# Joined record loads at the ends of both rounds, 384 more key columns kept, and small tiles put together, in a two-round decode kernel

## The chip, the core and the metric

The kernel runs on one core of a Trainium2 chip. The metric is the device time of one execution in microseconds (us); less is better. The time before is 711.71 us, the median of 3 runs (711.58 to 711.9).

The engines in the text: PE (TensorE, matrix products; its weight loads are PEld), DVE (VectorE), ACT (ScalarE), POOL (GpSimd), and SP, which here only issues transfers from HBM. The 16 DMA engines of the core carry them out in the order of issue.

## The reference

Four layers of decode for 4 sequences, one new token each: attention, MLP, attention, MLP, each with a layer norm ahead and a residual. Both attention layers read the same caches and weights, and so do both MLPs.

```python
def _A_ref(x, k_cache, v_cache, wq, wo):        # x 4 x 1 x 640, 32 heads of 128
    W = min(4096, max(256, Sk // 4))            # the last 1024 positions
    q = (x @ wq).reshape(B, Sq, Hq, Dh).transpose(0, 2, 1, 3)
    k, v = k_cache[:, :, Sk - W:, :], v_cache[:, :, Sk - W:, :]
    p = softmax(einsum("bhqd,bhkd->bhqk", q, k) * (Dh ** -0.5))
    o = einsum("bhqk,bhkd->bhqd", p, v)
    return o.transpose(0, 2, 1, 3).reshape(B, Sq, Hq * Dh) @ wo

def _B_ref(x, w1, w2):                          # 640 -> 1728 -> 640
    return maximum(x @ w1, 0) @ w2

x = x + _A_ref(layernorm(x), ...)
x = x + _B_ref(layernorm(x), ...)
x = x + _A_ref(layernorm(x), ...)
x = x + _B_ref(layernorm(x), ...)
```

All numbers are 32-bit floats.

## The kernel before

The host lays the data out as 32 records, one for each head: 128 partitions by 9,472 columns (REC). Columns 0 to 640 are the head's query weights (WQ), 640 to 4,736 the keys of the 4 sequences in two halves of 2,048 (K, VH), 4,736 to 8,832 the values (V), the last 640 the output weights (WO). A record is 4.85 MB, the 32 together 155 MB, and each of the two rounds (attention and MLP) reads them; SBUF holds little over five. MLP weights stand in an array of their own (`wm`): 8,640 columns of W1 in five blocks, then W2 in tiles of 160 columns.

SBUF is cut into `store` (five slots of a record, and FIRST = 2,176 columns ahead of them), `kept` and `ring`. In round 0 head h goes to slot h mod 5; the order is 0 to 31. Round 1 begins with heads 27 to 31, which are still in SBUF, and goes on with 0 to 26; the first FIRST columns of head 0 (its query weights and its first keys) also stay from round 0.

All loads are listed ahead, in one order (`items`), and SP issues them in that order. A load is issued as soon as all columns that it overwrites have been used: after each step `done` frees that step's columns and `pump` issues what has room. One load has one completion: a consumer of any of its columns waits for all of it. The sizes of the loads are written by hand:

- `GROUPS`: five heads in three loads (`FIVE`: 15,744, 15,872 and 15,744 columns); the last group of round 1, heads 19 to 23, in four (`LAST_FIVE`: 14,208, 14,208, 9,472, 9,472).
- `ending`: the last three heads of a round in pieces, query weights and keys (4,736 columns) apart from the values. In round 0 the WO parts of the last six heads come last of all.
- `MLP_RING`, `IN_RING`, `places`: the passage between the rounds, in which MLP weights go through `ring` and a parked part of the last slot (`park` copies 2,560 columns of head 31 to PSUM, `unpark` brings them back into the slot of head 27), and round 1's first loads go piecewise into whatever columns come free.
- `W1_SLOT`, `W2_SLOT`: the last MLP weights, into slots of round 1 that come free.

PE, DVE and ACT each keep the order in which the code is written (`InOrder`). One step of the loop over heads, with n counting and h the head: scores of the next head (8 matmuls into one of two `sc_ps` tiles), its maximum (DVE) and exponential (ACT), values of head h (8 matmuls into `o_ps`), `picks` (DVE: adds up the blocks of `o_ps`), query of the head after next (5 matmuls into `misc`), `output_T` (`t_ps`), `project` (4 matmuls into `acc`, the residual), then `weights` (DVE: transposes the exponentials into `wT`, the matmul operand). So a head's query is issued one step ahead of its scores and two ahead of its values. In the last step of a round, four filler matmuls (`busy`, `acc<-kept`) stand between the values of the third last head and the query of the last.

The MLP: five blocks of W1 (matmuls `sc_ps<-ring,xT` or `sc_ps<-store,xT`), the hidden layer through DVE (transposes, relu), then W2 (matmuls `acc<-...,scratch`). After the second MLP, DVE copies `acc` to SBUF and SP stores it.

## Time and profile before

| | |
|---|---|
| median of 3 runs | 711.71 us (711.58 to 711.9) |
| the profiled execution's own time | 712.25 us |
| its span in the profile | 710.5 us |
| PE busy | 513.0 us (72%) |
| DVE busy | 293.3 us (41%) |
| ACT busy | 99.7 us (14%) |
| moved | 301.96 MB, mean 425 GB/s |
| mean granted PE clock | 0.803 of full speed |

The span runs from the first to the last event of the profile; the time has 1.75 us more around it. Nearly all instructions are recorded by one helper, so lines of the code say little and groups are told by their tiles: `misc<-xT,store` is a query, `sc_ps<-store,qT` scores, `o_ps<-store,scratch` values. Each fp32 matmul shows as two records (x10 for the 5 of a query). In brackets behind a row stands the engine's idle time ahead of it and what ended it. PEclk is the share of full speed that PE was granted.

### The profile page before, as it was taken

The numbers are of one execution on the slowest core, as the hardware profiler recorded it, in microseconds if no ns is written. First come the engines' busy times: TensorE is split into PE (matmuls) and PEld (weight loads), VectorE is DVE, ScalarE is ACT, GpSimd is POOL, SyncE is SP. The second block draws the span as 40 slices with busy tenths as digits, with TensorE's granted clock in tenths as the row PEclk, the third lists the DMA queues.
The fourth block names the chain that finished last, engine by engine and source line by source line (L and its number), as shares of the span: only waits on it lengthen the run. The fifth ranks groups of instructions, "written<-read, shape, count | busy, mean of one in ns | idle before, by whom it ended". The sixth has DMA issues, their size and how long they took to land.

```text
span 710.5 us, 8480 instructions
## 1 busy us (share of the span) xinstructions
PE 513.0 (72%) x3722; PEld 214.0 (30%) x3722; DVE 293.3 (41%) x518; ACT 99.7 (14%) x210; POOL 1.1 (0%) x9
## 2 busy tenths in 40 slices
PE   0777586677584578869888999656584678686986
PEld 0332232232331223333323443222241232332322
DVE  3242353243342343435531775525162243453651
ACT  0110110011010110111120422101010011011110
POOL 0000000000000000000000000000000000000000
PEclk9977787677778776877999999968597677777989
DMA  9999999999999999999999999999999999999996
GB/s 398 439 416 447 425 435 443 414 439 450 418 435 441 424 437 421 423 439 423 430 398 403 412 426 433 445 435 437 431 435 426 438 436 430 432 432 416 433 425 281
DMA packets 12596, 301.96 MB, mean 425 GB/s; under 512 B 1408, under 2 KB 1552, under 8 KB 4624
## 3 DMA queue, kind: packets, MB, share of 16 engines
q1 hardware_dynamic: 12528, 301.42, 98.9%
q8 instruction: 29, 0.48, 0.2%
q14 instruction: 7, 0.06, 0.0%
q10 hardware_dynamic: 32, 0.01, 0.0%
HBM read 301.34 MB, written 0.08 MB: 424 GB/s over the span
## 4 chain that ended last, share of the span: by engine, by line
DMA 72%; PE 23%; DVE 4%; issue 1%; ACT 1%; ACTq 0%; SPq 0%; DVEq 0%
DMA store<-rec 65%; PE sc_ps L102 9%; PE o_ps L102 6%; DMA store<-wm 4%; PE acc L102 3%; PE misc L102 3%; DMA ring<-wm 2%; DVE scratch L102 2%; PE t_ps L102 1%; DVE o_ps L102 1%; ACT oTs L102 1%; DVE small L102 0%; DVE sc_ps L102 0%; ACT sc_ps L102 0%; ACTq L102 0%
## 5 line engine op out<-in xcount | busy, mean ns | idle before, releaser
L102 PE MATMUL sc_ps<-store,qT 128*32 128x512 f32 x1024 | 194.5, 849 | 35.7 <-DMA store<-rec 34.3
L102 PE MATMUL misc<-xT,store 128*128 128x4 f32 x620 | 95.6, 281 | 109.8 <-DMA store<-rec 109.8
L102 DVE TENSOR_REDUCE small<-sc_ps 128x1 f32<-128x1024 f32 x64 | 78.4, 1224 | 181.3 <-PE sc_ps L102 181.2
L102 PE MATMUL o_ps<-store,scratch 128*16 128x512 f32 x960 | 149.5, 701 | 1.7 <-DMA store<-rec 1.4
L102 PEld LDWEIGHTS misc<-xT,store 128*128 128x128 f32 x620 | 90.2, 227 | 166.6 <-DMA store<-rec 119.4
L102 ACT ACTIVATE sc_ps<-sc_ps,small 128x1024 f32<-128x1024 f32 x64 | 69.8, 1091 | 322.6 <-DVE small L102 322.6
L102 DVE STREAM_TRANSPOSE sc_ps<-sc_ps 128x1024 f32<-128x1024 f32 (+1 forms) x70 | 80.8, 1155 | 0.1
L102 PEld LDWEIGHTS sc_ps<-store,qT 128*32 128x32 f32 x1024 | 41.5, 139 | 112.4 <-issue 60.7
L102 PEld LDWEIGHTS o_ps<-store,scratch 128*16 128x16 f32 x960 | 33.8, 117 | 117.4 <-issue 107.8
L102 DVE TENSOR_TENSOR o_ps<-o_ps,of_block 128x512 f32<-128x512 f32 x62 | 43.3, 699 | 50.6 <-PE o_ps L102 50.6
L102 DVE TENSOR_TENSOR qT<-misc,rows 128x4 f32<-128x4 f32 x61 | 9.5, 155 | 112.9 <-PE misc L102 112.9
L102 PE MATMUL acc<-store,oTs 128*4 128x160 f32 x488 | 34.1, 363 | 17.0 <-ACT oTs L102 17.0
L102 DVE TENSOR_REDUCE scratch<-o_ps 128x128 f32<-128x512 f32 x62 | 42.9, 691 | 2.1
L102 ACT COPY oTs<-t_ps 128x4 f32<-128x4 f32 x59 | 9.6, 163 | 207.4 <-PE t_ps L102 207.4
L102 PE MATMUL t_ps<-rows,scratch 128*128 128x4 f32 x118 | 25.8, 289 | 11.3 <-DVE scratch L102 10.3
L102 PEld LDWEIGHTS t_ps<-rows,scratch 128*128 128x128 f32 x118 | 21.9, 231 | 17.4 <-DVE scratch L102 13.1
L102 DVE SCALAR_TENSOR_TENSOR scratch<-sc_ps,small,of_batch 128x128 f32<-128x128 f32 (+1 forms) x70 | 23.7, 339 | 3.5 <-PE o_ps L102 0.9
L102 PE MATMUL acc<-kept,small 128*1 128x328 f32 (+2 forms) x54 | 17.7, 433 | 0.0
L102 PEld LDWEIGHTS acc<-store,oTs 128*4 128x4 f32 x488 | 7.1, 84 | 22.5 <-ACT oTs L102 22.1
L102 ACT ACTIVATION_READ_ACCUMULATOR sc_ps<-sc_ps,small 128x1 f32 x64 | 12.3, 193 | 0.0
L102 DVE RECIPROCAL small<-small 128x1 f32<-128x1 f32 x64 | 9.8, 153 | 2.3 <-ACT sc_ps L102 2.3
L102 PE MATMUL acc<-store,scratch 128*4 128x160 f32 x146 | 6.1, 299 | 3.3 <-DMA store<-wm 3.2
(83 smaller groups left out, 99.8 us busy)
## 6 DMA issues: line engine op xcount, KB each, us to landing
store<-rec SPq DMA_DIRECT2D x14, 7872.0 KB, 27.3
store<-rec SPq DMA_DIRECT2D x7, 7936.0 KB, 29.9
store<-rec SPq DMA_DIRECT2D x4, 7104.0 KB, 30.8
store<-rec SPq DMA_DIRECT2D x11, 2368.0 KB, 36.5
store<-rec SPq DMA_DIRECT2D x3, 4736.0 KB, 25.7
store<-rec SPq DMA_DIRECT2D x2, 4416.0 KB, 29.1
store<-rec SPq DMA_DIRECT2D x3, 2048.0 KB, 40.7
store<-rec SPq DMA_DIRECT2D x1, 4160.0 KB, 21.6
```

What stands on the lines that cost most here:

```text
L102: r = build(*args, **kwargs)
```

## The change

Eight of 88 transfers go, by joins:

- Round 0, heads 25 and 26: the two records are stored interleaved in HBM (query weights and keys of 25, the same of 26, values and WO of 25, the same of 26), in both rounds. In round 0 the pair comes in one load up to column 16,256, with the rest of 26's values going to `kept` as before. Head 29 comes whole but for its WO.
- Round 1: heads 19 to 23 come as `FIVE`, 24 as one load, query weights and keys of 25 and 26 as one load. W1 of the second MLP comes in two loads instead of three.
- The passage: `unpark` lays the parked columns side by side, so that the free rest of head 27's keys is one stretch of 1,536 columns instead of 1,024 and 512; head 28's keys make room for one load of 4,096 instead of two of 2,048.

FIRST grows by 384 columns, paid for by smaller small tiles: `xT` keeps 32 columns, `scratch` 256; four tiles of four columns become `quads`. One score matmul of head 0 in round 1 is cut in two at the new border. The hidden layer is transposed inside PSUM and its used columns alone are written to `scratch`.

```diff
-FIRST = K + 3 * 512
+FIRST = K + 3 * 512 + 384
...
-IN_RING = [(2176, 4736, "spare", 0), (4736, 6272, "ring", 0), (6272, 8832, "ring", 1536)]
+IN_RING = [(FIRST, 4736, "spare", 0), (4736, 6272, "ring", 0), (6272, 8832, "ring", 1536)]
+PAIR = H - 7
+PAIRED = [(PAIR, 0, V, 0), (PAIR + 1, 0, V, V), (PAIR, V, REC, 2 * V), (PAIR + 1, V, REC, V + REC)]
-W1_SLOT = [[0, 1], [2, 3], [4]]
+W1_SLOT = [[0, 1, 2], [3, 4]]
-LAST_FIVE = [REC + 4736, 2 * REC - 4736, REC, REC]
-GROUPS = [{h: FIVE for h in range(0, 25, 5)}, {6: THREE, 9: FIVE, 14: FIVE, 19: LAST_FIVE}]
+GROUPS = [{h: FIVE for h in range(0, 25, 5)}, {6: THREE, 9: FIVE, 14: FIVE, 19: FIVE}]
...
-    xT = sb.tile([P, FD], F32, name="xT")
-    scratch = sb.tile([P, 480], F32, name="scratch")
+    xT = sb.tile([P, 32], F32, name="xT")
+    scratch = sb.tile([P, 256], F32, name="scratch")
...
+    def pair(r, lo, hi):
+        parts = [(("rec", r, h), x + max(lo - a, 0), min(y, x + hi - a), home(PAIR, r) + max(lo, a))
+                 for h, x, y, a in PAIRED if lo < a + y - x and a < hi]
+        load(rec, PAIR * REC + lo, PAIR * REC + hi, "store", home(PAIR, r) + lo, parts)
...
     def ending(r, hs, late):
         a, b, c = hs[-3:]
-        end = WO if late else REC
-        for h, lo, hi in ((a, 0, V), (b, 0, V), (a, V, end), (c, 0, V), (b, V, end), (c, V, WO if late else KEPT)):
-            piece(r, h, lo, hi)
-        if late:
+        if not late:
+            piece(r, a, 0, REC)
+            for lo, hi in ((0, 2 * V), (2 * V, V + REC), (V + REC, REC + KEPT)):
+                pair(r, lo, hi)
+        else:
+            for h, lo, hi in ((a, 0, WO), (b, 0, V), (c, 0, V), (b, V, WO), (c, V, WO)):
+                piece(r, h, lo, hi)
...
-        if h >= 25:
-            piece(0, h, 0, KEPT if h == LAST - 1 else WO if h >= H - LATE else REC)
-        if h == LAST - 1:
-            piece(0, h, KEPT, WO, "kept", 0)
+        if h == PAIR:
+            pair(0, 0, REC + KEPT)
+            piece(0, h + 1, KEPT, WO, "kept", 0)
+        elif h >= LAST:
+            piece(0, h, 0, WO)
...
-        a = b + (K, K + 512, K + VH, K + VH + 512, K + VH + 1024)[i]
+        a = b + K + 512 * i
...
-            dve.transpose(scratch[:, lo:hi], h_ps[:, lo:hi])
-            h = hT[:, lo // 32:hi // 32, :B]
+            dve.transpose(warm[:, lo:hi], h_ps[:, lo:hi])
+            h = warm[:, lo:hi].rearrange("p (m j) -> p m j", j=32)[:, :, :B]
...
+    rec[PAIR:PAIR + 2] = np.concatenate([rec[h, :, x:y] for h, x, y, _ in PAIRED], 1).reshape(P, 2, REC).swapaxes(0, 1)
```

How the loads stand on SP's queue at the end of round 1, before: heads 19 to 23 in four, then 24's keys, 25's keys, 24's values, 26's keys, 25's values, a part of 26's values, then the weights (a DMAHW name in a wait is a completion count of an earlier load, PE_49 a count of PE's steps).

```order
L102 DMA store<-rec 128x14208 [waits DMAHW3_49,PE_49]
L102 DMA store<-rec 128x14208 [waits DMAHW4_49,PE_49]
L102 DMA store<-rec 128x9472 [waits DMAHW5_49,PE_49]
L102 DMA store<-rec 128x9472 [waits PE_49]
L102 DMA store<-rec 128x4736 [waits DMAHW6_49]
L102 DMA store<-rec 128x4736 [waits PE_49] x2
L102 DMA store<-rec 128x4736 [waits DMAHW7_49,PE_49]
L102 DMA store<-rec 128x4736 [waits PE_49]
L102 DMA store<-rec 128x2048 [waits PE_49]
```

The same place now, from head 19's group on:

```order
L105 DMA store<-rec 128x15744 [waits DMAHW7_49,PE_49]
L105 DMA store<-rec 128x15872 [waits DMAHW0_49,PE_49]
L105 DMA store<-rec 128x15744 [waits DMAHW1_49,PE_49]
L105 DMA store<-rec 128x9472 [waits DMAHW2_49,PE_49]
L105 DMA store<-rec 128x9472 [waits DMAHW3_49,PE_49]
L105 DMA store<-rec 128x4736
L105 DMA store<-rec 128x2048 [waits PE_49]
```

The first 9,472 columns are head 24, the second the query weights and keys of 25 and 26 together; the columns in front of that load's end are the same as those in front of 26's keys before.

What PE does with them, before: the query of head 25 (the first `misc` row), with output and projection of head 23, 25's scores, 24's values, the fillers, the query of head 26 (`sc_ps_73` and `sc_ps_74` are the two score tiles, 70 and 71 in the changed kernel).

```order
L102 MATMUL misc<-xT,store 128x4 [waits DMAHW3_49]
L102 MATMUL t_ps<-rows,scratch 128x4 [waits DVE_49]
L102 MATMUL acc<-store,oTs 4x160 [waits Activation_49]
L102 MATMUL sc_ps_73<-store,qT 32x512 [waits DVE_49]
L102 MATMUL o_ps<-store,scratch 16x512 [waits DMAHW4_49,DVE_49]
L102 MATMUL acc<-kept,small 1x328 x4
L102 MATMUL misc<-xT,store 128x4 [waits DMAHW5_49]
```

And now (in both pieces the rows that only go on with the same matmul are left out):

```order
L105 MATMUL misc<-xT,store 128x4 [waits DMAHW6_49]
L105 MATMUL t_ps<-rows,scratch 128x4 [waits DVE_49]
L105 MATMUL acc<-store,oTs 4x160 [waits Activation_49]
L105 MATMUL sc_ps_70<-store,quads 32x512 [waits DVE_49]
L105 MATMUL o_ps<-store,scratch 16x512 [waits DVE_49]
L105 MATMUL acc<-kept,small 1x328 x4
L105 MATMUL misc<-xT,store 128x4 x5
```

The order of the matmuls is the same. The query of 25 waits for another load (the pair's); the waits of 24's values and of 26's query on loads are gone.

At the end of round 0, SP's queue before, from head 25 on (25, 26's first part, 26's rest to `kept`, 27, 28, then the pieces of 29 to 31):

```order
L102 DMA store<-rec 128x9472 [waits DMAHW5_49,PE_49]
L102 DMA store<-rec 128x6784 [waits DMAHW6_49,PE_49]
L102 DMA kept<-rec 128x2048
L102 DMA store<-rec 128x8832 [waits PE_49]
L102 DMA store<-rec 128x8832 [waits DMAHW7_49,PE_49]
L102 DMA store<-rec 128x4736
L102 DMA store<-rec 128x4736 [waits DMAHW0_49,PE_49]
L102 DMA store<-rec 128x4096 [waits PE_49]
L102 DMA store<-rec 128x4736 [waits DMAHW1_49,PE_49]
L102 DMA store<-rec 128x4096 [waits PE_49]
```

And now (the third 8,832 is head 29 whole, the 4,736 behind it the keys of 30 and of 31):

```order
L105 DMA store<-rec 128x16256 [waits DMAHW6_49,DMAHW5_49,PE_49]
L105 DMA kept<-rec 128x2048 [waits DVE_49]
L105 DMA store<-rec 128x8832 [waits PE_49]
L105 DMA store<-rec 128x8832 [waits DMAHW7_49,PE_49]
L105 DMA store<-rec 128x8832 [waits PE_49]
L105 DMA store<-rec 128x4736 [waits DMAHW0_49]
L105 DMA store<-rec 128x4736 [waits PE_49]
L105 DMA store<-rec 128x4096
```

Head 29's values moved ahead of 30's keys, and 25's record waits for the end of the load that also brings most of 26.

## Prediction

> **What bounds the kernel now.** I read the page first (span, slices, queues), then the chain of work that ended last, then the timeline of the engines at the places where the change edits the loads: the ends of the two rounds and the passage between them.

> ```profile
> span 710.5 us, 8480 instructions
> ...
> DMA  9999999999999999999999999999999999999996
> GB/s 398 439 416 447 425 435 443 414 439 450 418 435 441 424 437 421 423 439 423 430 398 403 412 426 433 445 435 437 431 435 426 438 436 430 432 432 416 433 425 281
> DMA packets 12596, 301.96 MB, mean 425 GB/s; under 512 B 1408, under 2 KB 1552, under 8 KB 4624
> ...
> q1 hardware_dynamic: 12528, 301.42, 98.9%
> ...
> DMA 72%; PE 23%; DVE 4%; issue 1%; ACT 1%; ACTq 0%; SPq 0%; DVEq 0%
> ```

> The 16 DMA engines are busy in every slice but the last, and the packets of SP's queue fill 98.9% of their time: the kernel is a stream of 301 MB. The chain at the end shows the same, with the rows of its last stretch in order of time (start, length, what):

> ```profile
> 635.80 37.16 DMA store<-rec
> 673.03 31.83 DMA store<-wm
> 704.90 2.83 PE acc L102 x68
> ```

> From 635.80 to 704.90 the end waits for bytes alone. But TensorE is only a little ahead there. Its timeline at the end of round 1 (start, busy us, what, idle time before it):

> ```profile
> 669.44 1.28 PE L102 MATMUL misc<-xT,store 128*128 128x4 f32 x10
> ...
> 672.05 1.90 PE L102 MATMUL sc_ps<-store,qT 128*32 128x512 f32 x16
> 673.77 1.90 PE L102 MATMUL o_ps<-store,scratch 128*16 128x512 f32 x16
> 675.48 2.37 PE L102 MATMUL acc<-kept,small 128*1 128x328 f32 x8
> 678.60 1.28 PE L102 MATMUL misc<-xT,store 128*128 128x4 f32 x10 [0.75 <-DMA store<-rec]
> ```

> In order: query of head 25, its scores, the values of head 24, four filler matmuls, and at 678.60 the query of head 26, which waits 0.75 us for its record. So head 25's work fits just into the time in which head 26's keys come.

> **The change, part by part.**

> *The end of round 1.* Before, heads 25 and 26 bring query weights and keys in a transfer each. Now one transfer of 9,472 columns brings both, and the query of head 25 waits for it. Behind it the queue holds the same columns in the same order of heads as before, and ahead of it too (24's keys, 25's keys, 24's values, 26's keys were 4 x 4,736 columns; now 2 x 9,472). So the joined transfer lands when 26's keys landed: TensorE saw them at 678.60. All that it did from 669.44 on now starts at 678.60. At full clock that is 675.48 + 2.37 - 669.44 = 8.4 us until the query of head 26 may start. But TensorE will come out of a wait there. Heads 19 to 23 now come in three transfers like the other groups, so the rest of 22 and all of 23 land together, where TensorE saw 23:

> ```profile
> 656.22 1.28 PE L102 MATMUL misc<-xT,store 128*128 128x4 f32 x10 [3.60 <-DMA store<-rec]
> ...
> 663.28 1.28 PE L102 MATMUL misc<-xT,store 128*128 128x4 f32 x10
> ```

> From 23's query to 24's took 7.1 us; the second half of 22's scores and 21's values (1.0 and 1.9 at full clock) come ahead of it, so 24's query is due near 667, and 24's whole record lands there too, where 25's keys did, some 11 us before the pair. Query, scores and values take 6.2 us (669.44 to 673.77 + 1.90). That leaves about 5 us idle. After an idle 2.35 us the trace shows this:

> ```profile
> 643.90 2.29 PE L102 MATMUL misc<-xT,store 128*128 128x4 f32 x10 [2.35 <-DMA store<-rec]
> ...
> 647.42 3.49 PE L102 MATMUL sc_ps<-store,qT 128*32 128x512 f32 x16
> 650.73 1.89 PE L102 MATMUL o_ps<-store,scratch 128*16 128x512 f32 x16
> ```

> The granted clock of these stretches (columns: stretch, length, busy time and count of PE, PEld, DVE, ACT, POOL, then PEclk, DMA share, GB/s):

> ```profile
> 643.79:650.62 6.83, 6.41 (x36) 3.68 (x40) 1.75 (x4) 0.16 (x1) 0.00 (x0) 0.50 1.00 433
> 660.86:681.34 20.48, 18.13 (x158) 7.88 (x154) 12.29 (x21) 3.94 (x8) 0.00 (x0) 1.00 1.00 428
> 681.34:688.16 6.82, 6.39 (x38) 1.48 (x34) 4.14 (x8) 1.37 (x3) 0.00 (x0) 0.50 1.01 429
> ```

> At half clock the same steps take 650.73 + 1.89 - 643.90 = 8.7 us, with the fillers (2.37, by then at full clock again) 11.1. I take 11.1, since the idle time is longer than in that row. So the query of head 26 starts 11.1 us late, at 689.7.

> How much of this the tail swallows, I read from what the tail waits for today:

> ```profile
> 684.30 3.61 PE L102 MATMUL o_ps<-store,scratch 128*16 128x512 f32 x16
> ...
> 700.28 0.19 DVE L102 SCALAR_TENSOR_TENSOR scratch<-scratch,rows 128x32 f32<-128x32 f32 x1
> 701.22 1.80 PE L102 MATMUL acc<-store,scratch 128*4 128x160 f32 x44 [1.29 <-DMA store<-wm]
> 704.90 2.79 PE L102 MATMUL acc<-store,scratch 128*4 128x160 f32 x68 [1.88 <-DMA store<-wm]
> ```
> ```profile
> 707.23 0.11 PEld L102 LDWEIGHTS acc<-store,scratch 128*4 128x4 f32 x8 [0.34 <-DMA store<-wm]
> ```

> The values of head 25 ran at half clock (3.61 against 1.90): 1.7 us come back if the clock stays full. The hidden layer is ready at 700.47 and the first W2 tiles land for 701.22: 0.7. The next wait is 1.88, the last 0.34. Sum 4.6 us; in the changed kernel all these bytes are there long before. So this part costs 11.1 - 4.6 = **+6.5 us** (3.8 if the clock stays full), and the chain at the end is TensorE's and VectorE's, no longer the DMA's.

> *Fewer transfers, fewer bytes.* 384 columns of 128 x 4 bytes are 196,608 bytes: at 425 GB/s 0.46 us. What a transfer costs the queue no row shows; 98.9% leaves 1.1% of 710.5 = 7.8 us outside packets, 0.09 for each of 88, and at the other end all the time above the fastest slice (301.42 MB at 450 GB/s are 670 us) would be 40.5/88 = 0.46. I take 0.09, as the share is of these very packets. Only what lies ahead of the joined pair counts now: 7 of the 8 transfers, and of these the four in round 0 and in the passage between the rounds (and the 0.46 of bytes) are taken back there, where the queue waits for room. The three behind it give **-0.3 us** (ends 0 and -3.7 = 7 x 0.46 + 0.46).

> *The passage between the rounds.* Head 28's keys come in two halves as room is freed at 394.78 and 395.64; joined, they go out at the second:

> ```profile
> 394.78 0.33 SPq L102 DMA_DIRECT2D store<-rec  x1
> ```
> ```profile
> 395.64 0.33 SPq L102 DMA_DIRECT2D store<-rec  x1
> ```
> ```profile
> 390.00:400.00 10.00, 9.51 (x74) 3.84 (x66) 8.41 (x20) 5.20 (x9) 0.00 (x0) 1.00 0.98 383
> ```

> This is the slowest 10 us of the middle, at 383 GB/s: the queue is nearly dry, so up to 0.86 us of the delay shows. It falls on a queue that comes 0.46 us early. I take **+0.3** (0 to 0.9). The room that 384 columns free adds nothing else: the extra split matmul is one of 0.2 us in a stretch where TensorE works ahead.

> *The end of round 0.* Head 29 comes whole (8,832 columns), behind it 30's keys, 31's keys; 25 and 26 come as one pair.

> ```profile
> 334.81 1.28 PE L102 MATMUL misc<-xT,store 128*128 128x4 f32 x10
> ...
> 340.38 1.28 PE L102 MATMUL misc<-xT,store 128*128 128x4 f32 x10
> ...
> 344.56 1.91 PE L102 MATMUL o_ps<-store,scratch 128*16 128x512 f32 x16 [0.26 <-DMA store<-rec]
> 346.27 2.37 PE L102 MATMUL acc<-kept,small 128*1 128x328 f32 x8
> 350.06 1.28 PE L102 MATMUL misc<-xT,store 128*128 128x4 f32 x10 [1.43 <-DMA store<-rec]
> ...
> 358.20 0.28 DVE L102 SCALAR_TENSOR_TENSOR scratch<-sc_ps,small,of_batch 128x64 f32<-128x64 f32 x1
> ...
> 359.87 3.06 PE L102 MATMUL sc_ps<-store,scratch 128*16 128x512 f32 x16 [2.45 <-DVE scratch L102]
> ```

> Before, 30's query ran at 340.38; now its keys land where 29's values did, 344.5. From query 30 to the last filler took 346.27 + 2.37 - 340.38 = 8.3 us: now 352.8 instead of the landing at 350.06, so 31's query is 2.7 late. The values of head 31 had 359.87 - 358.48 = 1.4 us of slack, and their matmuls ran 3.06 at half clock where 1.9 is the full price, so 1.2 more may come back: +0.1 to +1.3 at full clock, and some 3 us more if the 4 us of idle before 29's query (its record lands near 339) halve the clock. I take **+0.5** (0 to 4). It moves the first MLP weights' release and with it the queue.

> *Small tiles.* xT, scratch and the four-column tiles change places; the hidden layer is transposed within PSUM and compacted to SBUF. Same count of instructions, a handful of waits of VectorE on itself. **0** (-0.2 to +0.3).

> Sum: 6.5 - 0.3 + 0.3 + 0.5 = +7.0. The profiled execution's own time is 712.25 (span 710.5 and 1.75 around it): 719.2. The runs' median 711.71 lies 0.54 below it: **718.7 us**.

> **The rivals.**

> *The clock stays full* at 678.60: the stretch 660.86 to 681.34 is granted 1.00 with an idle 0.75 in it. Then 3.8 in place of 6.5: 716.0. Against it: the idle time is several times as long.

> *Round 0's end is paid in full*: half clock there too, +3.5 in place of +0.5: 721.7. Against it: the stretch was at full clock, with little idle; now about 4 us come before 29's query.

> *The queue gains more than it shows (faster).* Place: each completed transfer ahead of the joined pair. Were a transfer worth 1.0 us, the pair would land 7.5 us early, at 671.1, the query of head 26 would follow at full clock at 679.5, less than 4.6 late, and the weights would be in 8.5 us early; the end would be at 671.1 + 8.4 + 27.3 = 706.8 (31.9 - 4.6 = 27.3 is the tail from that query), so 708.0. It decides from (8.4 - 4.6 - 0.46)/7 = 0.48 us a transfer, and that is above the upper end of 0.46. Against it: 98.9%.

> [...]

> *That the change isn't what it says* falls away: SP's queue holds 79 transfers where it held 87 (ScalarE's queue one in both), and 384 columns fewer are loaded.

> **How the numbers follow.** Forecast case 50% (716.5 to 721), full clock 20% (714.3 to 716.5), round 0 paid in full 15% (721 to 723), gains of the queue 7%, tail slack far larger than 4.6 so that little is left 8% (half of it within 0.2%). 0.2% is 1.4 us, about what a measurement of this kernel tells from no change. Leaving out the last two and the top of the third: 714.3 to 722.0. Faster 0.08, same 0.05, slower 0.87.

> **What would show it.** In the profile after: a row of the query of head 25 that waits on DMA store<-rec near 678, idle some 5 us before, and PEclk 0.50 behind it; no DMA wait any more at the last W2 tiles; the chain of the last 30 us on PE and DVE; a last slice of the DMA row well under 6. In round 0, a wait of some 4 us near 339 and 31's query near 353. I am wrong if the query of head 26 starts before 683, or if the last tiles still wait for store<-wm.

## The result, and the profile after

The changed kernel takes 717.89 us (median of 6 runs, 716.37 to 719.55) where the kernel before took 711.83 in the same session: a ratio of 1.0084, 95% interval 1.0072 to 1.0097. The forecast was 718.7 in 714.3 to 722.0. The profiled run took 717.87 (span 716.2).

The page of the changed kernel, the rows that answer to those of before:

```profile
span 716.2 us, 8466 instructions
...
DMA  9999999999999999999999999999999999999993
GB/s 395 453 395 447 447 417 433 443 439 419 439 443 426 424 444 433 412 441 424 424 402 387 402 436 426 453 429 446 425 430 444 421 428 441 442 414 418 425 428 164
...
q1 hardware_dynamic: 11376, 301.22, 98.1%
```

The transfers still fill the span, but for the last slice: 3 tenths at 164 GB/s, against 6 at 281. The bytes are in and the kernel goes on. The chain that ended last, its end in order of time (start, length, what):

```profile
646.67 32.49 DMA store<-rec
...
679.20 1.93 PE misc L105 x10
...
682.57 3.41 PE sc_ps L105 x16
685.99 2.01 PE o_ps L105 x16
688.00 2.20 PE acc L105 x8
...
705.08 3.42 PE sc_ps L105 x34
708.51 4.85 PE acc L105 x115
```

Before, two transfers made up this stretch up to 704.90. Now the last one on the chain is the pair, and from 679.20 on TensorE carries it, with short pieces of VectorE and ScalarE between. TensorE's timeline in the same place:

```profile
656.78 1.07 PE L105 MATMUL sc_ps<-store,quads 128*32 128x512 f32 x3 [8.48 <-DMA store<-rec]
...
662.05 1.51 PE L105 MATMUL misc<-xT,store 128*128 128x4 f32 x10
...
668.16 1.28 PE L105 MATMUL misc<-xT,store 128*128 128x4 f32 x10
...
672.46 1.90 PE L105 MATMUL o_ps<-store,scratch 128*16 128x512 f32 x16
679.20 1.93 PE L105 MATMUL misc<-xT,store 128*128 128x4 f32 x10 [4.84 <-DMA store<-rec]
...
687.83 2.37 PE L105 MATMUL acc<-kept,small 128*1 128x328 f32 x8
690.13 1.28 PE L105 MATMUL misc<-xT,store 128*128 128x4 f32 x10
...
709.31 3.98 PE L105 MATMUL acc<-store,scratch 128*4 128x160 f32 x112
```

The rest of 22 at 656.78, 23's query at 662.05, 24's at 668.16, then 4.84 us of waiting for the pair, 25's query at 679.20 and 26's at 690.13 instead of 678.60. The last W2 matmuls wait for no transfer any more.

### The profile page after: what moved, and what is told of

Same layout as the page of the kernel before. It is cut to its first block, busy times and chain, and to the rows that moved or that the text cites. A ratio compares the mean times of both kernels' runs of the same rounds, so it can differ in the third digit from the quotient of the medians.

```text
span 716.2 us, 8466 instructions
## 1 busy us (share of the span) xinstructions
PE 497.3 (69%) x3724; PEld 210.8 (29%) x3724; DVE 293.6 (41%) x518; ACT 99.6 (14%) x210; POOL 1.1 (0%) x9
## 4 chain that ended last, share of the span: by engine, by line
DMA 68%; PE 25%; DVE 4%; ACT 1%; issue 1%; ACTq 0%; SPq 0%; DVEq 0%
DMA store<-rec 65%; PE sc_ps L105 9%; PE o_ps L105 7%; PE acc L105 4%; PE misc L105 4%; DMA ring<-wm 3%; DVE scratch L105 2%; DVE o_ps L105 2%; PE t_ps L105 2%; ACT oTs L105 1%; DVE small L105 0%; ACT sc_ps L105 0%; DVE sc_ps L105 0%; ACTq L105 0%; SPq L102 0%
## 5 line engine op out<-in xcount | busy, mean ns | idle before, releaser
L105 PE MATMUL sc_ps<-store,quads 128*32 128x512 f32 (+1 forms) x1026 | 184.6, 807 | 52.4 <-DMA store<-rec 51.0
L105 DVE STREAM_TRANSPOSE sc_ps<-sc_ps 128x1024 f32<-128x1024 f32 (+3 forms) x74 | 82.7, 1117 | 12.2 <-PE sc_ps L105 12.0
L105 PEld LDWEIGHTS sc_ps<-store,quads 128*32 128x32 f32 x1026 | 40.9, 137 | 123.8 <-DMA store<-rec 59.8
L105 DVE TENSOR_TENSOR o_ps<-o_ps,quads 128x512 f32<-128x512 f32 x62 | 43.4, 699 | 48.6 <-PE o_ps L105 48.6
L105 DVE TENSOR_TENSOR quads<-misc,rows 128x4 f32<-128x4 f32 x61 | 9.5, 156 | 121.5 <-PE misc L105 121.5
L105 PE MATMUL t_ps<-rows,scratch 128*128 128x4 f32 x118 | 25.7, 288 | 11.1 <-DVE scratch L105 11.0
L105 DVE SCALAR_TENSOR_TENSOR scratch<-sc_ps,small,quads 128x128 f32<-128x128 f32 (+1 forms) x70 | 23.8, 340 | 2.7
```

The costliest lines, as they stand in the source:

```text
L105: r = build(*args, **kwargs)
```

## The experiments

Times are medians; ratios are to runs of the kernel before in the same session (medians 711.83 for the change, 712.02 for the next four rows, 711.87 for the four after them, 712.22 for the last four). A ratio is worked out over all runs and is not the quotient of the two medians: they differ by up to 0.05%. Where two kernels of the table are compared, their ratios are subtracted, and the interval of the difference is taken as the root of the sum of the squares of the two.

| kernel | us | ratio (95%) |
|---|---|---|
| the change | 717.89 | 1.0084 (1.0072 to 1.0097) |
| pair's keys in two | 714.49 | 1.0030 (1.0018 to 1.0042) |
| 19 to 23 in four, pair kept | 718.38 | 1.0087 (1.0070 to 1.0105) |
| whole end of round 1 as before | 714.42 | 1.0032 (1.0015 to 1.0049) |
| fillers ahead of the pair | 716.99 | 1.0071 (1.0052 to 1.0090) |
| passage, 384 columns, tiles only | 712.98 | 1.0021 (1.0005 to 1.0037) |
| 384 columns and tiles only | 712.19 | 1.0004 (0.9994 to 1.0014) |
| round 1's end as before, fillers in round 0 | 714.40 | 1.0037 (1.0021 to 1.0054) |
| before, 45 transfers more | 713.47 | 1.0020 (1.0012 to 1.0029) |
| tiles and head 29 whole | 713.44 | 1.0012 (1.0003 to 1.0022) |
| tiles and the 4,096 load | 712.61 | 1.0008 (0.9999 to 1.0017) |
| the change, three joins undone | 712.59 | 1.0004 (0.9993 to 1.0014) |
| the change, no fillers in round 1 | 717.13 | 1.0073 (1.0061 to 1.0085) |

**The pair in two loads.**

```diff
-            for lo, hi in ((0, 2 * V), (2 * V, V + REC), (V + REC, REC + KEPT)):
+            for lo, hi in ((0, V), (V, 2 * V), (2 * V, V + REC), (V + REC, REC + KEPT)):
```

> One part of the change undone: in round 1 the 9,472 columns with the query weights and keys of heads 25 and 26 come in two transfers of 4,736 again; all else is the changed kernel (717.89). Theory (the joined pair makes the query of 25 wait for the keys of 26): 25's keys land 5.6 us ahead of 26's, at 679.2 - 5.6 = 673.6, when TensorE ends the values of 23 (674.3). No idle time, full clock, the query of 26 at 674.3 + 8.4 = 682.7, and from there 26.1 us (716.2 - 690.1) to 708.8. But the last weights land at 707.5 and the tail behind them is 3.6, so the stream of transfers sets the end again at 711.1 + 1.7 = 712.8 us (712.0 to 713.3). Rival A (the loss comes from heads 19 to 23 in three loads, so that 24 is late, and from the late room for the weights): stays above 716. Rival B (it comes from the passage or from round 0): stays near 717.9.

Measured 714.49: one cut takes back 0.54% (3.8 us) of the 0.84%. The place of the larger part of the loss is the pair. The time expected, 712.8, was missed. The timeline of the profiled run, which at 715.60 was the longest of twelve (712.30 to 715.60):

```profile
659.09 1.07 PE L105 MATMUL sc_ps<-store,quads 128*32 128x512 f32 x3 [6.77 <-DMA store<-rec]
...
677.71 1.28 PE L105 MATMUL misc<-xT,store 128*128 128x4 f32 x10
...
680.45 3.45 PE L105 MATMUL sc_ps<-store,quads 128*32 128x512 f32 x16
...
687.74 1.28 PE L105 MATMUL misc<-xT,store 128*128 128x4 f32 x10
...
706.92 3.98 PE L105 MATMUL acc<-store,scratch 128*4 128x160 f32 x112
```

25's query waits for nothing here, but comes at 677.71, not 674.3, with 25's scores at half clock (3.45 for 1.90). TensorE, and not the stream, still sets this end. But the large loads for heads 19 to 24 explain little of the lost time: the kernel with three joins undone, further below, keeps them, takes the same 10.0 us from 25's query to 26's, and is at 712.59. What differs is that the rest of 22 comes at 656.11 there and at 659.09 here. Most of the missed time was lost ahead of this place, where the other two of those three joins stand.

**Heads 19 to 23 in four loads, the pair kept.**

```diff
+LAST_FIVE = [REC + 4736, 2 * REC - 4736, REC, REC]
-GROUPS = [{h: FIVE for h in range(0, 25, 5)}, {6: THREE, 9: FIVE, 14: FIVE, 19: FIVE}]
+GROUPS = [{h: FIVE for h in range(0, 25, 5)}, {6: THREE, 9: FIVE, 14: FIVE, 19: LAST_FIVE}]
```

> Another part undone alone: heads 19 to 23 of round 1 come in the old four transfers (14,208, 14,208, 9,472, 9,472 columns); the pair stays joined. Theory: 24's work is done earlier, but the query of 25 still waits for the joined pair, which lands at 679.2 less at most 0.6 (the queue runs dry for some 0.5 us ahead of the third of the three loads); the wait grows from 4.8 to some 8 or 9 us and the rest is unchanged: 717.3 us (716.6 to 718.1). Rival A (three loads for 19 to 23 are the cause): 712 to 713.5.

Measured 718.38, nothing gained, and just above the range expected. The queries of 25 and 26:

```profile
681.88 1.28 PE L106 MATMUL misc<-xT,store 128*128 128x4 f32 x10 [2.37 <-DMA store<-rec]
...
691.39 1.28 PE L106 MATMUL misc<-xT,store 128*128 128x4 f32 x10
```

The pair came later in this run, and all behind it with it: while the pair is joined, work done earlier ahead of it only waits. The one wait of 8 or 9 us that was expected was two, 4.03 us ahead of 24's query (at 670.71), since 24 still comes whole, and 2.37 ahead of 25's.

**The whole end of round 1 as before.** `LAST_FIVE` as above, W1 in three loads, and:

```diff
-            piece(r, a, 0, REC)
-            for lo, hi in ((0, 2 * V), (2 * V, V + REC), (V + REC, REC + KEPT)):
+            piece(r, a, 0, V)
+            pair(r, 0, V)
+            piece(r, a, V, REC)
+            for lo, hi in ((V, 2 * V), (2 * V, V + REC), (V + REC, REC + KEPT)):
                 pair(r, lo, hi)
```

> The whole end of round 1 undone (heads 19 to 23 in four transfers, the keys of 24, 25 and 26 apart, first W1 blocks of the last MLP in three loads); the joins at the end of round 0 and in the passage, the 384 columns and the small tiles stay. It also asks whether these parts by themselves gain. Theory: the stream of transfers sets the end as before. In the changed kernel it stands 0.35 us behind the kernel before when both have brought the same data of round 1 (mean landing 451.54 against 451.19), so 711.83 + 0.35 = 712.2 us (711.7 to 712.7). Rival (fewer transfers and bytes gain as counted in the sum, four transfers at 0.09 and 0.46 us of bytes): 711.0 us.

Measured 714.42, the same as with the pair alone undone. The last W2 matmuls wait for transfers again (2.38 and 1.90 us), so the stream sets the end. The other three joins at this end (19 to 23, 24, W1) thus cost nothing beside the pair that can be told, but some 0.3% is lost elsewhere, more than the 0.35 us expected.

**Fillers in the wait for the pair.**

```diff
             picks(0)
+            if r and n == H - 4:
+                for _ in range(6):
+                    busy()
             query(r, hs[n + 2], n + 2)
```

> The changed kernel with six filler matmuls (0.6 us each by the row of the four fillers, 2.37) between the values of head 23 and the query of head 25, in the 4.84 us in which TensorE waits for the pair. Nothing else moves. Theory (the clock fell to half because of the idle time, and that is 2.7 us of the loss): idle falls to some 1.3 us, the granted clock stays 1.00 behind it, the query of 26 starts at 679.2 + 8.4 = 687.6 in place of 690.1, and the time is 717.9 - 2.5 = 715.4 us (715.0 to 716.2). Rival (the clock falls whatever the idle time, or VectorE sets the pace of these steps): 717.9.

The profiled run (715.63) went as expected: the idle time is 1.02, the clock stays full (1.00 from 670.80 to 687.87), and 26's query follows 7.82 us behind 25's, not 10.93.

```profile
680.06 1.28 PE L105 MATMUL misc<-xT,store 128*128 128x4 f32 x10 [1.02 <-DMA store<-rec]
...
687.88 1.28 PE L105 MATMUL misc<-xT,store 128*128 128x4 f32 x10
```

Three of six runs stand at 715.6 to 715.9, three at 718.0 to 719.0, so the median, 716.99, gained only 0.13%, which the intervals don't part from none. No profile of the later three was taken; why they are longer stays open.

**Passage, 384 columns and tiles only.** All loads at both round ends and the layout of 25 and 26 as before.

> The joins at the ends of both rounds undone (all loads there, and the layout of heads 25 and 26, as before); left of the change are the two joins in the passage, the 384 columns and the small tiles. Theory (the part of the change that is left in the experiment with the old end of round 1 loses at the end of round 0): the passage costs the +0.35 us read from the landings at 451, 712.0 + 0.35 = 712.3 us (711.8 to 712.9). Rival (the passage or the small tiles carry the 2.4 us that were measured there): 714 or more.

**384 columns and tiles only.** The two joins of the passage undone as well.

> All joins undone: of the change only the 384 columns of head 0 that stay and the small tiles (with the hidden layer transposed in PSUM) are left; the loads are those of the kernel before, one of them 384 columns shorter (and 384 columns moved between two others). Theory: 196,608 bytes less are 0.46 us, and the tiles cost nothing: 711.5 us (711.1 to 712.1), a ratio of 0.9994. Rival (the tiles cost: VectorE works from PSUM, tiles share a place): 712.5 or more.

Measured 712.98 and 712.19. The tiles and the shorter load make no difference that can be told (0.9994 to 1.0014): the 0.46 us of bytes can't be seen in the runs. With the passage joined it is 0.17% more, 1.2 us (0.8 by the medians); the interval, 0.19% to a side, also allows nothing. In one of the twelve runs of the first of these two kernels, the profiled one, it was 719.3 (columns as in the prediction: stretch, length, busy time of PE, PEld, DVE, ACT, POOL, PEclk, DMA share, GB/s):

```profile
385.00:395.00 10.00, 8.91 (x58) 4.64 (x58) 1.69 (x7) 0.00 (x0) 0.00 (x0) 0.60 0.87 339
395.00:405.00 10.00, 9.65 (x52) 4.01 (x52) 6.63 (x15) 4.46 (x8) 0.00 (x0) 0.55 0.47 138
```

The same stretches of the kernel before:

```profile
385.00:395.00 10.00, 8.91 (x92) 4.81 (x93) 4.92 (x15) 3.51 (x7) 0.00 (x0) 1.00 1.00 401
395.00:405.00 10.00, 9.60 (x84) 3.49 (x76) 7.71 (x14) 3.03 (x7) 0.00 (x0) 1.00 1.01 410
```

Here TensorE frees the room for each load. It is as busy as in the kernel before (9.65 us of 10 against 9.60), but at about half the clock, and the queue is starved: 138 GB/s. Whether the joins had a part in this fall of the clock isn't shown.

**Fillers in round 0.** The kernel with round 1's end as before, and:

```diff
+            if not r and n == H - 5:
+                for _ in range(6):
+                    busy()
             query(r, hs[n + 2], n + 2)
```

> The experiment with the old end of round 1 (714.4) again, with six filler matmuls (3.6 us at full clock) in round 0 ahead of the query of head 29, where TensorE waited 5.25 us for the whole record of 29 and came out at a granted clock of 0.50. Theory (the end of round 0 is paid because of the clock: 31's query came at 355.1 there, against 351.5 in the profile of the changed kernel, which ran at full clock, and the fourth MLP load went out at 366.1 instead of 362.8): with the idle time cut to some 1.7 us the clock stays 1.00, 31's query comes at about 351.5, and the time falls by 1.5 to 2 us, to 712.6 us (712.2 to 713.2). Rival (the loss lies in the passage or the tiles): 714.4.

The theory fell: 714.40. In the profile the idle time was 1.39, yet the scores behind it took 3.20 us, where the next ones (347.62) took 1.92:

```profile
338.82 1.28 PE L106 MATMUL misc<-xT,store 128*128 128x4 f32 x10 [1.39 <-DMA store<-rec]
...
340.36 3.20 PE L106 MATMUL sc_ps<-store,quads 128*32 128x512 f32 x16
...
353.38 1.28 PE L106 MATMUL misc<-xT,store 128*128 128x4 f32 x10
```

Even with the idle time cut to 1.39 us, from the fillers' end at 337.43 on, these scores were not at full speed (the last section has more on this). 31's query came 1.7 us earlier than without the fillers (353.38 against 355.06), but the time is the same. What the clock in round 0 costs by itself stays open.

**45 transfers more.** The kernel before with:

```diff
+    def quarters(h, sizes):
+        ends = [sum(sizes[:i]) + sizes[i] * q // 4 for i in range(len(sizes)) for q in (1, 2, 3, 4)]
+        ends = [max(g * REC + x for g in range(6) for x in CUTS if g * REC + x <= e) for e in ends]
+        return [b - a for a, b in zip([0] + ends, ends)]
...
-            group(0, h, GROUPS[0][h])
+            group(0, h, quarters(h, GROUPS[0][h]))
```

> The kernel before with the 15 loads of heads 0 to 24 in round 0 cut into four each: 45 transfers more, the same bytes in the same order. It measures what a transfer costs the queue. Theory (0.09 us each, from the queue's share of 98.9%; the packets' own durations in the trace, some 8 ns more for each of 8 packets and a 9 ns packet at the end, give 0.07): head 24's last load lands 3.2 to 4.1 us later than at 283.0 and the time is 715.0 to 716.0 us. [...] No change at all would say that a transfer in a full queue is free.

The queries of heads 27 and 28 wait for their records in both kernels. Before:

```profile
317.60 2.30 PE L102 MATMUL misc<-xT,store 128*128 128x4 f32 x10 [3.99 <-DMA store<-rec]
328.02 1.28 PE L102 MATMUL misc<-xT,store 128*128 128x4 f32 x10 [0.69 <-DMA store<-rec]
```

With 45 more transfers:

```profile
319.46 2.29 PE L102 MATMUL misc<-xT,store 128*128 128x4 f32 x10 [5.50 <-DMA store<-rec]
329.88 1.28 PE L102 MATMUL misc<-xT,store 128*128 128x4 f32 x10 [1.35 <-DMA store<-rec]
```

Both are 1.86 us later: 0.04 us a transfer, half of the theory's 0.09. The time says the same, 1.60 us or 0.036 each; its interval (0.12% to 0.29%) gives 0.02 to 0.05. That the landings agree so well with it is in part luck: in the profile with head 29 whole alone, further below, where the loads ahead are as before, 27's query came at 318.06, after a wait of 7.37.

**Head 29 whole, alone; the 4,096 load, alone.** Each on top of the kernel with 384 columns and tiles only; the first with the order of loads of the changed kernel for heads 29 to 31, the second with

```diff
-(1, K, 1, K + VH), (1, K + VH, 1, V),
+(1, K, 1, V),
```

> One join alone on top of the experiment with the small tiles and the 384 columns (all other loads as before, 712.2): in round 0 head 29 comes in one load of 8,832 columns, ahead of the keys of 30 and 31. Theory: the query of 29 waits for the values of 29 too (338.7 instead of 334), what TensorE had ahead there is lost, and where the wait leaves a clock slot of 3.4 us mostly idle, the next slots run at half clock; the park copies and the fourth MLP load go out later: +1.4 us, the difference between the experiment with all of round 0's joins and the passage (714.4) and the passage's alone (713.0): 713.5 us (712.7 to 714.4). Rival (the joined pair 25 and 26 in round 0 carries it, or nothing does and the difference is noise): 712.2.

> Another join alone on the same base (712.2): the keys of head 28's old place are filled by one load of 4,096 columns instead of two of 2,048. Theory: the first half of the room comes free 0.86 us ahead of the second, the queue there is nearly dry, so up to 0.86 us is lost: 712.8 us (712.4 to 713.3), and now and then more, when TensorE's clock falls in the passage. Rival (the other join of the passage, 1,024 and 512 to 1,536, or noise): 712.2.

Head 29 whole: 713.44, 0.08% (0.6 us) above its base, half of the 1.4 expected. The 4,096 load: 0.04% (0.3 us). With 0.14% to a side, neither can be told from nothing by itself. The first one's profile shows what it does to TensorE, a wait of 5.25 us, and behind it scores in 3.64 us, where the next ones (349.38) took 1.92:

```profile
338.89 2.29 PE L103 MATMUL misc<-xT,store 128*128 128x4 f32 x10 [5.25 <-DMA store<-rec]
...
341.54 3.64 PE L103 MATMUL sc_ps<-store,quads 128*32 128x512 f32 x16
...
355.13 1.28 PE L103 MATMUL misc<-xT,store 128*128 128x4 f32 x10
```

**Three joins undone.** The changed kernel with the pair's keys in two, head 29 in keys and values in the old order, and the 4,096 columns as two loads.

> The changed kernel with three of its joins undone: the pair's keys in round 1 (two loads of 4,736), head 29 in round 0 (keys and values apart, in the old order) and the 4,096 columns of the passage (two of 2,048). The other five joins stay (83 transfers). Theory (these three make TensorE or the queue wait, the other five are free and gain nothing that can be measured, at some 0.04 us a transfer): 712.2 us, like the small tiles alone (711.6 to 712.8). Rival (the other joins lose as well: heads 19 to 23 in three loads, the W1 blocks in two, the pair in round 0): 713.5 or more. If fewer transfers gain after all: under 711.3, and it would beat both kernels.

Measured 712.59, a ratio of 1.0004. Three of the joins carry all of the loss that can be told; the other five together neither cost nor gain more than the interval, 0.1% or 0.8 us to a side. Against the kernel with the pair's keys alone in two (1.0030), the other two joins, head 29 and the 4,096 columns, are worth 0.26% (1.9 us), with 0.16% to a side: together they do cost, though neither showed it by itself. The end of round 1 in the profile:

```profile
656.11 1.07 PE L105 MATMUL sc_ps<-store,quads 128*32 128x512 f32 x3 [6.65 <-DMA store<-rec]
...
675.04 1.28 PE L105 MATMUL misc<-xT,store 128*128 128x4 f32 x10
...
685.08 1.28 PE L105 MATMUL misc<-xT,store 128*128 128x4 f32 x10
...
704.26 3.98 PE L105 MATMUL acc<-store,scratch 128*4 128x160 f32 x112
```

TensorE sets the end here too, but with 25's query at 675.04 it does so at a span of 711.4, next to the stream's 710.5. It doesn't beat the kernel before, and no experiment points to a version that would.

**No fillers in round 1.**

```diff
-            if end:
+            if end and not r:
                 for _ in range(4):
```

> The changed kernel without the four filler matmuls of round 1, which stand between the values of 24 and the query of 26. Theory (after the pair has landed every piece of TensorE's work up to the end is on the path, the fillers with 2.2 us too): 717.9 - 2.2 = 715.7 us (715.2 to 716.7). Rival (VectorE, DMA or the clock set the time behind the pair, or the clock falls without the fillers and takes it back): 717.9.

Measured 717.13, above the range expected: 0.11% below the change, where 2.2 us are 0.31%. With 0.17% to a side that can't be told from nothing. The profile:

```profile
680.06 2.30 PE L105 MATMUL misc<-xT,store 128*128 128x4 f32 x10 [4.63 <-DMA store<-rec]
...
689.21 1.28 PE L105 MATMUL misc<-xT,store 128*128 128x4 f32 x10
```

From 25's query to 26's it takes 9.15 us, 1.8 less than the 10.93 of the change: in this profile they are on the path. The time shows less; in this run the pair came 0.86 later, which takes back about half.

## Why the prediction was right, point by point

*The joined pair makes 25's query wait, and the end passes from the stream to TensorE.* Shown. It landed where 26's keys landed (679.20, forecast 678.6), after 4.84 us of idle (forecast about 5), and cutting it in two takes back 3.8 us. In these profiles the time from 26's query to the end of the span is nearly one constant when TensorE sets the end:

| kernel | 25's query | 26's query | span | 26's query to end |
|---|---|---|---|---|
| before | 669.44 | 678.60 | 710.5 | 31.9 (stream) |
| the change | 679.20 | 690.13 | 716.2 | 26.1 |
| pair's keys in two | 677.71 | 687.74 | 713.9 | 26.2 |
| 19 to 23 in four | 681.88 | 691.39 | 717.5 | 26.1 |
| fillers ahead | 680.06 | 687.88 | 713.9 | 26.0 |
| no fillers | 680.06 | 689.21 | 715.4 | 26.2 |
| three joins undone | 675.04 | 685.08 | 711.4 | 26.3 |

*The clock.* Forecast: half clock behind the wait, 11.1 us to 26's query, 8.4 if full. Measured 10.93 and, in the experiment that kept the clock full, 7.82. That rival (full clock at the pair) is refuted for the profiled run of the change by the stretches of its clock:

```profile
672.75:676.16 3.41, 1.61 (x16) 0.23 (x8) 2.58 (x3) 1.20 (x2) 0.00 (x0) 1.00 0.93 400
676.16:679.58 3.42, 0.38 (x4) 0.38 (x4) 0.00 (x0) 0.00 (x0) 0.00 (x0) 1.00 0.94 404
679.58:682.99 3.41, 3.10 (x23) 2.38 (x26) 1.75 (x4) 0.16 (x1) 0.00 (x0) 0.51 0.96 409
682.99:686.40 3.41, 3.41 (x20) 0.72 (x16) 0.35 (x1) 0.00 (x0) 0.00 (x0) 0.50 1.06 448
686.40:689.81 3.41, 3.41 (x24) 0.89 (x16) 2.27 (x3) 1.21 (x2) 0.00 (x0) 0.99 1.00 428
```

Two of the change's six runs, 716.37 and 716.58, stand about where that rival put the time, 716.0. There is no profile of them, so whether the clock stayed full there is open.

*The tail's slack.* This term was mis-sized: the tail swallowed 31.9 - 26.1 = 5.8 us, not 4.6, so the end of round 1 costs 10.9 - 5.8 = 5.1 in the profile, not 6.5 (the span grew by 5.7, since the pair landed 0.6 later than 26's keys had). The rows on VectorE that end the first half of the hidden layer, before and now:

```profile
699.49 0.19 DVE L102 SCALAR_TENSOR_TENSOR scratch<-scratch,rows 128x28 f32<-128x28 f32 x1
709.06 0.19 DVE L105 SCALAR_TENSOR_TENSOR scratch<-sc_ps,rows 128x28 f32<-128x28 f32 x1
```

From 26's query to the end of this row it took 699.68 - 678.60 = 21.1 us and now takes 709.25 - 690.13 = 19.1. These 2.0 us are put down to the clock, which was at 0.50 in part of that stretch before (681.34 to 688.16; taken as 1.7). The other 3.8 are the waits for W2, taken as 2.9. The working let W2 begin when the whole hidden layer is ready (700.47), but its first matmuls need only this half: the first wait is 1.5 us and not 0.7. That is 0.8 of the missing 0.9. The difference of the ratios (the change less its old end, 0.52%) gives 3.7 us for the end of round 1; the intervals, 0.13% and 0.17% to a side, allow either.

*Fewer transfers.* -0.3 forecast; at 0.04 us each the three that count are -0.1. The rival in which the queue gains is refuted; it needed 0.48 a transfer, and 45 more cost 1.60 us together.

*The passage.* +0.3 forecast. Measured 0.17% (1.2 us) for both joins and 0.04% for the larger one alone, neither clear of its interval, so the size isn't settled. What the working didn't consider is a run in which TensorE's clock falls there, the 719.3 above (0.60 and 0.55 of full speed).

*The end of round 0.* +0.5 (0 to 4) forecast; the runs give 0.08% and, with all joins there, 0.11%: 0.6 to 0.8 us, with 1.0 and 1.7 us to a side, so that no loss at all is allowed too. In the profile of the change it came cheaply:

```profile
328.14 2.29 PE L105 MATMUL misc<-xT,store 128*128 128x4 f32 x10 [2.58 <-DMA store<-rec]
...
338.56 1.28 PE L105 MATMUL misc<-xT,store 128*128 128x4 f32 x10 [2.12 <-DMA store<-rec]
...
351.45 1.28 PE L105 MATMUL misc<-xT,store 128*128 128x4 f32 x10
```

28's work had run at half clock (0.50 from 328.05 to 334.88), so the wait for 29 was 2.12, and the clock stayed full behind it (1.00 from 334.88 to 437.28). That is the exception: in all six other profiles with head 29 whole and no fillers there (the pair in two; 19 to 23 in four; round 1's end as before; fillers ahead of the pair; head 29 alone; no fillers in round 1) the wait was 4.9 to 5.3, 29's scores behind it took 3.64 us (30's 1.92), and 31's query came at 354.8 to 355.4. The row of it with round 1's end as before:

```profile
355.06 1.28 PE L106 MATMUL misc<-xT,store 128*128 128x4 f32 x10
```

So of the two ways that the prediction gave for this place, TensorE mostly goes the one of the rival, "paid in full". The rival's price was wrong: 31's query is some 5 us late against 350.06, and the time shows 0.6 to 0.8 and not 3.5, which lies outside both intervals. That the size came out near the forecast is luck: it was worked out for the way that TensorE mostly doesn't go. Where the other 4 us are swallowed, no run here isolates.

*Small tiles.* 0 forecast, +0.04% measured, within its interval of nothing.

By the runs the parts are 0.3 (tiles and bytes), 1.2 (passage), 0.8 (round 0), 3.7 (end of round 1): 6.0 of the forecast 7.0. Only the last of these is clear of its interval by itself (1.5 us to a side); head 29 whole (round 0) and the 4,096 columns (passage) are so only together, by the 1.9 us of the experiment with three joins undone. The forecast was right by its mechanism, the pair. That the total came so near is in part luck: an end of round 1 taken too large and the other parts taken too small partly cancel.

## What to carry to other kernels

In this kernel a transfer has one completion, so joining two loads moves the first consumer to the landing of the last byte (25's query from 669.44 to 679.20, behind a wait of 4.84); in its full queue a transfer saved gives back next to nothing (45 more cost 0.04 us each). Before joining, look at the consumer of the earlier half: how much work it does before the later half is due, and how much slack lies behind it, counted to the first instruction that needs the data and not to the last. Here TensorE was only a little ahead of the stream, and the small loads near the end of a round were what kept it ahead.
